# A linear-attention and mixture-of-experts kernel: the mask of the scores ahead of the second operands, another order of loads, and a shorter first layer in two places

## The chip, the cores and the metric

The kernel runs on one core of one Trainium2 chip. The metric is the device time in microseconds (us). Below, PE is the matmul engine, PEld its weight loads, DVE the vector engine, ACT the scalar engine, POOL the GpSimd engine and SP the engine that issues most of the transfers.

## What is computed

A gated recurrence over 4 batches of 768 steps with 8 heads of 48 numbers, then a layer of 8 experts in which each of the 3072 rows goes to the one expert that its gate prefers. Everything is float32.

```python
for t in range(S):                                   # S = 768
    state = alpha[:, :, t, :, None] * state + k[:, :, t] (outer) v[:, :, t]
    y[:, :, t] = q[:, :, t] @ state
x = y as 3072 rows of 384                            # 4 x 768 rows, 8 heads x 48
logits = x @ w_gate                                  # 8 experts
e = argmax(logits); gate = softmax(logits)[e]
out = gate * (relu(x @ w1[e]) @ w2[e])               # w1: 384 x 1024, w2: 1024 x 384
```

## The kernel before, in words

**Attention.** The rows are worked in 24 tiles of 128 steps, six to a batch. For a tile `s` the kernel takes the logarithm of alpha (`logs`, ACT, L326), sums it along the steps with a triangular matmul (`cums`, PE, L337, into one bank named `cum`), and takes two exponentials of the sums on ACT: `icp` (L340) and `cp` (L341, tile `cpb`). `operands` multiplies the keys with `icp` (L360) and the queries with `cp` (L362) into `kqb`, mostly on POOL. `transposes` (PE, L369) turns both, ACT (L374) and DVE (L372) copy them out as `kT` and `qT`. `scores` (PE, L382) makes the 128x128 scores of the even heads in `sA` and of the odd heads in `sB`; DVE masks `sA` into `dA` (L386), ACT copies `sB` into `dB` (L388), and POOL masks `dB` in place (L389). `weighs` (PE, L426) multiplies the scores with the values, `reads` (PE, L414) adds what the state `U` holds, `products` (PE, L448) and `state` (POOL, L463 and L465) carry the state on; no state is carried over the end of a batch, so some passes have half the reads or half the products. `rows` (PE, L474), `keep_rows` (ACT L481, POOL L482) and `store_rows` (SP, L487) turn the result to rows with their gate numbers and write them to DRAM.

The program order is written by hand: each engine runs its instructions in the order in which the code names them. The main loop takes two tiles a pass, `s` = 2, 4, ... 20. A pass takes the results of tiles s and s+1, the logarithms, sums and operands of s+5 and s+6, the transposes of s+3 and s+4, the scores of s+2 and s+3 and the rows of s and s+1. Its second half, in the code's order, ends so:

```python
            more_loads(5)
            do(decay_in, s + 4)
            rows(s + 1)
            keep_rows(s + 1)
            do(operands, s + 6)
            ...
            scores(s + 3)
            store_rows(s)
```

**Loads.** Every load and row store of the loop goes through SP's one queue, in program order. A list `to_load` fixes the order of the loads from tile 7 on; before, it is alpha of tile x+1, keys and queries of tile x, values of tile x-2, over and over. A pass takes 2, 2 and 5 loads from it, with the row stores and small transfers of the decay in between. One load is 192 KB, in pieces of 192 bytes. Keys, queries and alpha have five buffers each, the values six. Below, "k8" is the keys of tile 8, "a10" the alpha of tile 10.

**Routing.** As groups of four tiles are done, `choose` picks each row's expert on DVE, POOL adds up one-hot rows (`ohs`, L500), and two small products on PE (L505 and L506, `rank_products`) give each row its rank within its expert. From these come the lists of rows to gather.

**Experts.** The 8 experts are worked one after the other in 8 places of fixed size, `caps` = 448, 384, 448, 384, 416, 416, 416, 416 rows; expert 0 takes the first place and the others theirs by their counts after 20 tiles (`nth_of`). Rows are gathered in blocks of 128 that may straddle two places (POOL, L269), turned on PE (L960), put through `layer1` (PE, L968: 8 parts of 128 hidden numbers, each over 3 parts of the row, with the place's rows as columns; the relu on DVE and ACT, L973 and L975), and through `layer2` (PE, L984; scaled by the gate on ACT, L989; scattered to the output by POOL, L990). An expert with more rows than its place has all rows past a threshold `XR` done again in extra blocks of 128 rows, in a loop at the end that runs as often as `extra_blocks` counts; `room` holds the places' sizes for that count.

Of the kernel before, what the change touches and what calls it, by code (L numbers as in the profile page):

```python
# [18 lines left out]
def kernel(  # L19
# [29 lines left out]
    nc = tc.nc  # L49
    B, H, S, D = q.shape  # L50
    C = 128
# [21 lines left out]
    nth_of = (5, 0, 6, 1, 2, 3, 4)  # L73
    begins = [sum(caps[:i]) for i in range(E + 1)]
    NBK = begins[-1] // C
    CAP = max(caps)

    XR = min(caps)
    NX = -(-(N - XR) // C)
    assert E == 8 and begins[-1] % C == 0 and NX <= 32 and all(c % UN == 0 and c <= NU * UN for c in caps)  # L80

# [11 lines left out]
    EC = EB * C  # L93
# [82 lines left out]
    def late_consts(i):  # L176
        if i == 0:
            nc.gpsimd.memset(lt_strict[:], 1.0)
            nc.gpsimd.affine_select(
                lt_strict[:], lt_strict[:], compare_op=ALU.is_gt, fill=0.0,  # L180
                base=0, pattern=[[1, C]], channel_multiplier=-1,
            )
            nc.gpsimd.memset(ones_sq[:], 1.0)
        if i == 1:
            nc.gpsimd.memset(zero_e[:], 0.0)
            nc.gpsimd.memset(zero_w[:], 0.0)
        if 2 <= i < 9:
            for ti, tf, pattern, base, mult in list(iotas.values())[2 * (i - 2) : 2 * (i - 1)]:
                n = 1
                for _, m in pattern:  # L190
                    n *= m
                if n < ti.shape[1]:
                    nc.gpsimd.memset(ti[:, n:], -1)
                nc.gpsimd.iota(ti[:, :n], pattern=pattern, base=base, channel_multiplier=mult)
                nc.gpsimd.tensor_copy(tf[:], ti[:])
            if i == 2:
                nc.gpsimd.tensor_copy(ohs[:, 0, :], ohs0[:])
        p = i - 9
        if 0 <= p < E - 1:
            nc.gpsimd.memset(nth[:, p : p + 1], float(nth_of[p]))  # L200
            nc.gpsimd.memset(room[:, p : p + 1], float(caps[p + 1]))

    e_d = nc.dram_tensor("decay_rows", (NT // 2 + 1, 2 * H * DP), F32, kind="Internal").ap()
    x_d = nc.dram_tensor("x_rows", (N + 1, W), F32, kind="Internal").ap()
# [30 lines left out]
    w_t = {}  # L235
# [51 lines left out]
    with tc.tile_pool(name="ld", bufs=6) as ld, \  # L287
# [21 lines left out]
        def some_loads(names):  # L309
# [3 lines left out]

        to_load = [
            (n, x + d) for x in range(7, NT + 2)
            for n, d in ((("a", 1), ("k", 0), ("q", 0), ("v", -2)) * 2)[3 * (x > 7) :][:4]
        ]


# [283 lines left out]
        def do(f, i, *a):  # L603
            if 0 <= i < NT:
                f(i, *a)
# [90 lines left out]
        for s in range(2, NT - 2, 2):  # L696
            more_loads(2)
            if s == 2:
                store_rows(0)
            do(decay_out, s + 4)  # L700
            more_loads(2)

            for _ in range(8 if s > NT - 8 else 0):
                next(parts, None)
            y = results_of(s)
            reads(s)
            reads(s + 1)

            weighs(s, 0)
            weighs(s, 1)  # L710
            products(s + 1)
            products(s + 2)
            weighs(s + 1, 0)
            results_to(s, y, 0)
            weighs(s + 1, 1)
            results_to(s, y, 1)
            state(s + 1)
            do(logs, s + 5)
            if hots:
                one_hots(hots.pop(0))  # L720
            scores(s + 2)
            do(logs, s + 6)
            do(cums, s + 5)
            ranks = y[0][:].rearrange("r i p t -> r (i p t)")
            ranked = [rank_products(g, ranks[:, : len(g) * E]) for g in groups_of if g[-1] == s - 1]
            counts = ranks[:, C : C + E]
            if s in (TE, ORD):

                nc.tensor.matmul(
                    counts, lhsT=ones_sq[:], rhs=ohs[:, s, :], start=True, stop=True, skip_group_check=True,  # L730
                )
            if s == ORD:
                early_slots(ranks[:, 2 * C : 2 * C + EB * NQ])
                fetch_lot(0)
            for r in ranked if s < ORD else ():
                slots_of(*r)
            transposes(s + 3)
            do(operands, s + 5)
            state(s + 2)
            rows(s)  # L740
            keep_rows(s)
            store_rows(s - 1)
            if s == ORD:
                for r in ranked:
                    slots_of(*r)
                key = standing(counts[0:1, :])
                one_hots(hots.pop(0))
                one_hots(hots.pop(0))
                route = rps.tile([C, Dm], F32, name="cum")
                tokens_of_slots(0, TE)  # L750
            do(cums, s + 6)
            do(transposes, s + 4)
            more_loads(5)
            do(decay_in, s + 4)
            rows(s + 1)
            keep_rows(s + 1)
            do(operands, s + 6)
            if s == TE:
                close_early(counts[0:1, 0:1])
            scores(s + 3)  # L760
            store_rows(s)
            if s == 2:

                nc.sync.dma_start(x_d[N // 2 : N // 2 + 1, :], zero_w[:])
            late_consts(s + 2)
            late_consts(s + 3)
            if s == ORD:
                choose(groups_of[-2])
            if hots:
                one_hots(hots.pop(0))  # L770
            for g in groups_of[:-2]:
                if g[-1] == s + 1:
                    choose(g)
            for _ in range(4 if s == NT - 8 else 0):
                next(parts, None)
# [96 lines left out]
    def extra_blocks():  # L872

        cnt = sm.tile([1, E], F32)
        nc.vector.tensor_tensor(cnt[:], tot[:], rank0[:], op=ALU.subtract)
        og = sm.tile([1, E, NX], F32)
        nc.vector.tensor_tensor(
            og[:], cnt[:].unsqueeze(2).to_broadcast([1, E, NX]), thr[:, None, :].to_broadcast([1, E, NX]), op=ALU.is_gt,
        )
        ovt = sm.tile([1, E], F32)  # L880
        nc.vector.reduce_sum(ovt[:], og[:], axis=AX)
        sq = [1, E - 1, E - 1]
        own = sm.tile(sq, F32)
        nc.vector.tensor_tensor(
            own[:], stand[:].unsqueeze(2).to_broadcast(sq), nth[:, None, :].to_broadcast(sq), op=ALU.is_equal,
        )
        nc.vector.tensor_tensor(own[:], own[:], room[:, None, :].to_broadcast(sq), op=ALU.mult)
        cap = sm.tile([1, E], F32)
        nc.vector.memset(cap[:, :1], float(caps[0]))
        nc.vector.reduce_sum(cap[:, 1:], own[:], axis=AX)  # L890
        nc.vector.tensor_tensor(cap[:], cnt[:], cap[:], op=ALU.is_gt)
        nc.vector.tensor_tensor(ovt[:], ovt[:], cap[:], op=ALU.mult)
        ove = sm.tile([1, E], F32)
        nc.vector.tensor_tensor_scan(ove[:], ovt[:], zero_e[0:1, :], 0.0, op0=ALU.add, op1=ALU.add)
        ovs = sm.tile([1, E], F32)
        nc.vector.tensor_sub(ovs[:], ove[:], ovt[:])
        kx_b = kx[0:1, :].unsqueeze(2).to_broadcast([1, NX, E])

        def per(v):
            return v[0:1, None, :].to_broadcast([1, NX, E])  # L900

        ended = sm.tile([1, NX, E], F32)
        nc.vector.tensor_tensor(ended[:], per(ove), kx_b, op=ALU.is_le)
        xf = sm.tile([1, 2 * NX + 1], F32)
        nc.vector.reduce_sum(xf[:, :NX], ended[:], axis=AX)
        nc.vector.tensor_scalar_min(xf[:, :NX], xf[:, :NX], float(E - 1))

        at_x = sm.tile([1, NX, E], F32)
        nc.vector.tensor_tensor(at_x[:], kx_b, per(ovs), op=ALU.subtract)
        live = sm.tile([1, NX, E], F32)  # L910
        nc.vector.tensor_scalar(live[:], at_x[:], scalar1=0.0, scalar2=None, op0=ALU.is_ge)
        nc.vector.tensor_tensor(live[:], live[:], ended[:], op=ALU.subtract)
        nc.vector.tensor_tensor(at_x[:], at_x[:], per(xcol), op=ALU.add)
        nc.vector.tensor_tensor(at_x[:], at_x[:], live[:], op=ALU.mult)
        nc.vector.reduce_sum(xf[:, NX : 2 * NX], at_x[:], axis=AX)
        nc.vector.tensor_copy(xf[:, 2 * NX :], ove[0:1, E - 1 :])
        nc.vector.tensor_copy(xe[:], xf[:])
# [121 lines left out]
    for i in range(E):  # L1039
        if i == 0:  # L1040
            go_ahead(9)
            for k in range(EB, needed[0][-1] + 1):
                turn_block(k)
                go_ahead(3)
            go_ahead(99)
            layer1(w_t[0][0], xT[0], h_t[0], EC, caps[0])
        else:
            if i == E - 1:

                nc.gpsimd.drain()  # L1050
            h_t[i] = (wk if i % 2 else early).tile([C, FB, CAP], F32, name="h_sb", bufs=1)
            layer1(w_t[i][0], xT[i], h_t[i], 0, caps[i])

        coming = list(needed[i + 1]) if i + 1 < E else []
        for k in coming[:2]:
# [75 lines left out]
```

## Time and profile before

| | us |
|---|---|
| time, median of 4 runs (lowest, highest) | 431.84 (431.72, 432.11) |
| the profiled execution: its time | 433.72 |
| the profiled execution: its span in the trace | 431.8 |
| PE busy | 422.4 |
| DVE, ACT, POOL busy | 140.8, 108.4, 140.4 |
| second layer, matmuls (L984) | 137.1 |
| first layer, matmuls (L968) | 125.1 |

A profile is one execution. The busy time of an engine says how full it is, not whether it sets the end: for that one looks at what PE, the fullest one here, waited for. The row of the granted clock (PEclk) tells in tenths at what share of its full speed PE was allowed to run in each fortieth of the span. The attention takes about the first 141 us, the routing and the gathers up to about 160 us, the experts the rest.

### The profile page before, as it was taken

The page shows a single profiled execution, that of the slowest core. Times are in us where ns is not written, and L with a number is a line of the kernel's source. Part 1 is how long each engine was busy: PE and PEld are TensorE (multiplying, and loading weights), DVE is VectorE, ACT ScalarE, POOL GpSimd, SP SyncE. Part 2 cuts the span into 40 slices and gives each one's busy share as a digit, 9 for nine tenths or more (in the row PEclk, how much of TensorE's full clock was granted, in tenths as well). Part 3 has the DMA queues.
Part 4 walks back from the last instruction along what each step waited for, and adds up shares of the span by engine and source line. Part 5 has one row for each costly group of instructions (what it writes and reads, how often), then busy time and mean ns, then how long its engine had stood idle before and what let it go on. Part 6 is the DMA issues. An engine that isn't in the chain of part 4 may idle for free.

```text
span 431.8 us, 7708 instructions
## 1 busy us (share of the span) xinstructions
PE 422.4 (98%) x2990; PEld 286.6 (66%) x2990; DVE 140.8 (33%) x414; ACT 108.4 (25%) x230; POOL 140.4 (33%) x254
## 2 busy tenths in 40 slices
PE   8999899999999999999999999999999999999995
PEld 6887788888889888555555555655655455555452
DVE  6434457575767843721012101201201101111100
ACT  4565354555552321110111111011110110011011
POOL 5395577666655250160160110024010010010011
PEclk9999699999999999999999999999999999999999
DMA  9999999899986232995542710624530050000000
GB/s 158 185 166 199 199 197 187 177 191 194 189 220 204 99 99 80 395 397 170 193 113 58 266 40 10 250 86 120 212 116 18 2 182 20 0 32 20 1 33 29
DMA packets 132576, 59.43 MB, mean 138 GB/s; under 512 B 114614, under 2 KB 127452, under 8 KB 132538
## 3 DMA queue, kind: packets, MB, share of 16 engines
q1 hardware_dynamic: 127720, 48.96, 44.8%
q0 software_dynamic: 3328, 9.94, 7.1%
q8 instruction: 24, 0.39, 0.4%
q10 hardware_dynamic: 1490, 0.02, 0.2%
q14 instruction: 14, 0.11, 0.1%
HBM read 49.32 MB, written 9.98 MB: 137 GB/s over the span
## 4 chain that ended last, share of the span: by engine, by line
PE 63%; issue 28%; POOL 5%; DMA 2%; POOLq 0%; ACT 0%; DVE 0%; SPq 0%; DVEq 0%
PE zp L984 16%; PE hp L968 14%; PE sA L382 6%; PE y L426 5%; PE tp L369 5%; PE xr L474 5%; PE cum L337 4%; POOL out_dram L990 3%; PE y L414 2%; PE xr L612 2%; PE xtp L960 1%; PE sB L448 1%; POOL xg L269 1%; PE hp L785 1%; DMA k_sb<-in_k_dram 1%
## 5 line engine op out<-in xcount | busy, mean ns | idle before, releaser
L984 PE MATMUL zp<-w,h_sb 128*128 128x384 f32 (+2 forms) x560 | 137.1, 487 | 0.0
L968 PE MATMUL hp<-xT,w 128*128 128x416 f32 (+3 forms) x384 | 125.1, 486 | 0.0
L984 PEld LDWEIGHTS zp<-w,h_sb 128*128 128x128 f32 (+2 forms) x560 | 73.6, 163 | 56.3 <-issue 14.8
L968 PEld LDWEIGHTS hp<-xT,w 128*128 128x128 f32 x384 | 71.8, 190 | 51.8 <-issue 37.8
L990 POOL DMA_INDIRECT out_dram<-zo,o_idx x26 | 25.8, 992 | 219.2 <-ACT zo L989 214.2
L973 DVE TENSOR_SCALAR h_sb<-hp 128x416 f32<-128x416 f32 (+3 forms) x32 | 17.9, 558 | 149.2 <-PE hp L968 149.2
L989 ACT ACTIVATE zo<-zp,gw 128x384 f32<-128x384 f32 x26 | 15.1, 580 | 123.7 <-PE zp L984 119.1
L975 ACT ACTIVATE h_sb<-hp 128x416 f32<-128x416 f32 (+3 forms) x32 | 15.7, 490 | 107.3 <-PE hp L968 107.3
L382 PE MATMUL sA<-qT,kT 48*128 48x128 f32 x192 | 28.6, 291 | 0.2 <-DVE qT L372 0.2
L269 POOL DMA_INDIRECT xg<-x_rows,g_idx x26 | 25.1, 965 | 11.1 <-issue 6.4
L382 PE MATMUL sB<-qT,kT 48*128 48x128 f32 x192 | 28.6, 291 | 0.0
L962 DVE COPY xT<-xtp 128x384 f32<-128x384 f32 (+3 forms) x29 | 13.1, 485 | 44.3 <-PE xtp L960 44.2
L426 PE MATMUL y<-dB,vb 128*64 128x128 f32 x192 | 25.5, 279 | 2.1 <-POOL dB L389 2.1
L382 PEld LDWEIGHTS sA<-qT,kT 48*128 48x128 f32 x192 | 24.0, 193 | 4.9 <-issue 2.2
L360 POOL TENSOR_TENSOR kqb<-k_sb,icp 128x384 f32<-128x384 f32 x23 | 23.0, 1000 | 12.0 <-ACT icp L340 8.2
L426 PE MATMUL y<-dA,vb 128*64 128x128 f32 x192 | 26.6, 279 | 0.0
L369 PE MATMUL tp<-ident,kqb 128*128 128x128 f32 x192 | 26.2, 280 | 0.2 <-POOL kqb L362 0.2
L369 PEld LDWEIGHTS tp<-ident,kqb 128*128 128x128 f32 x192 | 22.6, 144 | 5.3 <-issue 2.7
L474 PE MATMUL xr<-back,yT 128*128 128x104 f32 x192 | 25.5, 277 | 0.0
L474 PEld LDWEIGHTS xr<-back,yT 128*128 128x128 f32 x192 | 24.1, 195 | 0.8 <-ACT xs L481 0.2
L382 PEld LDWEIGHTS sB<-qT,kT 48*128 48x128 f32 x192 | 24.0, 193 | 0.0
L372 DVE COPY qT<-tp 128x512 f32<-128x512 f32 x24 | 16.6, 690 | 20.4 <-PE tp L369 20.3
(178 smaller groups left out, 436.6 us busy)
## 6 DMA issues: line engine op xcount, KB each, us to landing
w<-in_moe_w_dram SPq DMA_DIRECT2D x14, 1536.0 KB, 6.7
x_rows<-xs SPq DMA_DIRECT2D x24, 196.0 KB, 3.4
a_sb<-in_alpha_dram SPq DMA_DIRECT2D x24, 192.0 KB, 4.1
k_sb<-in_k_dram SPq DMA_DIRECT2D x24, 192.0 KB, 3.8
q_sb<-in_q_dram SPq DMA_DIRECT2D x24, 192.0 KB, 4.5
vb<-in_v_dram SPq DMA_DIRECT2D x24, 192.0 KB, 3.8
w<-in_moe_w_dram SPq DMA_DIRECT2D x12, 128.0 KB, 4.1
w<-in_moe_w_dram SPq DMA_DIRECT2D x8, 192.0 KB, 3.9
```

The costliest lines, as they stand in the source:

```text
L269: nc.gpsimd.indirect_dma_start(out=xg[:, j, :], out_offset=None, in_=x_d[: N + 1 if n else TE * C + 1, :], in_offset=bass.IndirectOffsetOn ...
L337: nc.tensor.matmul(cum[:], lhsT=cmask[:], rhs=d["ln"][:], start=True, stop=True)
L360: k.tensor_tensor(kq[:, 0, :, :D], d["k"][:], heads(d["icp"]), op=ALU.mult)
L369: nc.tensor.transpose(tp[:, p, :], pair(kqb[s % 4][:, i], p), ident[:])
L372: nc.vector.tensor_copy(d[n][:], tp[:])
L382: nc.tensor.matmul(t[:, p, :], lhsT=d["kT"][r : r + D, p, :], rhs=d["qT"][r : r + D, p, :], start=True, stop=True,)
L426: nc.tensor.matmul(d["y"][h][at(p, a) : at(p, a) + DP, n, :], lhsT=d["v"][:, 2 * p + a, :], rhs=d["d" + "AB"[a]][:, p, :], start=(first an ...
L474: nc.tensor.matmul(xr[:, p, :], lhsT=d["yT"][:, p // (NP // 2), p % (NP // 2), :], rhs=back[:, p, :], start=True, stop=True)
L968: nc.tensor.matmul(hp[:, c0:c1], lhsT=w1[:, a, f * C : (f + 1) * C], rhs=xT[:, a, c0:c1], start=(a == 0), stop=(a == DB - 1),)
L973: nc.vector.tensor_relu(h[:, f, c0:c1], hp[:, c0:c1])
L984: nc.tensor.matmul(zp[i * wd : (i + 1) * wd, :], lhsT=h[:, f, c : c + wd], rhs=w2[:, f, :], start=(f == 0), stop=(f == FB - 1), skip_group ...
L990: ins = nc.gpsimd.indirect_dma_start(out=out[:, :], out_offset=bass.IndirectOffsetOnAxis(ap=idx, axis=0), in_=zo[:], in_offset=None, bound ...
```

## The change

Four things change.

1. In each pass of the loop `operands(s + 6)` stands after `scores(s + 3)`. On POOL the mask of `dB` (L389) of tile s+3 thereby stands ahead of the two products (L360, L362) of tile s+6. It changes the order in the passes s = 2 to 16, in which tiles s+6 are left; no other engine's order changes by it.
2. From tile 8 on the list of loads is keys of x, values of x-2, alpha of x+1, queries of x. From the second row store of the first pass on, SP's loads are then k8, v6, a9, q8, k9, v7, a10, q9, k10, v8, a11, q10, k11, v9, a12, q11, ... in place of v6, a9, k8, q8, v7, a10, k9, q9, v8, a11, k10, q10, v9, a12, k11, q11, ...; how many loads stand between the stores stays the same.
3. A list `cols` holds the columns of the first layer: 368 in the fourth place (of 384) and 400 in the eighth (of 416). The place keeps its gather, its turns and its second layer. POOL sets the hidden rows past the columns to zero ahead of the two first layers.
4. What counts as too many rows for a place is taken from `cols`; the threshold `XR` of the extra blocks goes from 384 to 256, and their greatest number from 21 to 22, so that some constants and the small operations that count the extra blocks get 22 columns in place of 21.

```diff
+    cols = (448, 384, 448, 368, 416, 416, 416, 400)
     CAP = max(caps)
-    XR = min(caps)
+    XR = min(cols) // C * C
     NX = -(-(N - XR) // C)
...
-            nc.gpsimd.memset(room[:, p : p + 1], float(caps[p + 1]))
+            nc.gpsimd.memset(room[:, p : p + 1], float(cols[p + 1]))
...
         to_load = [
             (n, x + d) for x in range(7, NT + 2)
-            for n, d in ((("a", 1), ("k", 0), ("q", 0), ("v", -2)) * 2)[3 * (x > 7) :][:4]
+            for n, d in (
+                (("a", 1), ("k", 0), ("q", 0), ("v", -2)) if x == 7 else (("k", 0), ("v", -2), ("a", 1), ("q", 0))
+            )
         ]
...
             keep_rows(s + 1)
-            do(operands, s + 6)
             if s == TE:
                 close_early(counts[0:1, 0:1])
             scores(s + 3)
+            do(operands, s + 6)
             store_rows(s)
...
-        nc.vector.memset(cap[:, :1], float(caps[0]))
+        nc.vector.memset(cap[:, :1], float(cols[0]))
...
-            layer1(w_t[0][0], xT[0], h_t[0], EC, caps[0])
+            layer1(w_t[0][0], xT[0], h_t[0], EC, cols[0])
...
-            layer1(w_t[i][0], xT[i], h_t[i], 0, caps[i])
+            if cols[i] < caps[i]:
+                nc.gpsimd.memset(h_t[i][:, :, cols[i] : caps[i]], 0.0)
+            layer1(w_t[i][0], xT[i], h_t[i], 0, cols[i])
```

## The prediction, made before the change was run

> **What bounds the kernel now.** I read the page first: the busy row, then the clock row.
>
> ```profile
> PE 422.4 (98%) x2990; PEld 286.6 (66%) x2990; DVE 140.8 (33%) x414; ACT 108.4 (25%) x230; POOL 140.4 (33%) x254
> PEclk9999699999999999999999999999999999999999
> ```
>
> PE is the bound from end to end, so an edit counts only if it removes a hole in PE, a stretch of slow clock, or PE work. One slice, the fifth (43.2 to 54.0 us), has a clock of 0.6. So next PE's own order of time, then the windows around that place (columns: stretch; its length, then busy us of PE, PEld, DVE, ACT, POOL; granted clock; DMA share; GB/s).
>
> ```profile
> 44.57 0.32 PE L426 MATMUL y<-dB,vb 128*64 128x128 f32 x1 [2.06 <-POOL dB L389]
> ```
>
> ```profile
> 43.00:44.00 1.00, 0.00 (x0) 0.00 (x0) 0.00 (x0) 0.13 (x1) 1.00 (x2) 1.00 0.76 183
> 45.00:46.00 1.00, 1.00 (x14) 0.67 (x9) 0.69 (x1) 0.00 (x0) 0.85 (x6) 0.60 0.87 167
> 51.00:52.00 1.00, 1.00 (x6) 1.00 (x6) 0.79 (x2) 0.23 (x1) 1.00 (x2) 0.50 1.01 183
> 52.00:53.00 1.00, 1.00 (x8) 0.82 (x7) 0.33 (x2) 0.11 (x1) 0.71 (x3) 0.99 1.10 208
> ```
>
> PE idles once for 2.06 us (the other holes of the loop are 0.2 us), and after it the clock is 0.5 from 45.2 (0.60 over the slice from 45 means 0.2 us at full) to 52.0: 6.8 us at half speed, 3.4 us lost. Check: from the first weighing matmul of pass s=4 (40.74) to that of s=6 (56.66) are 15.92 us; the same pass shape at s=10 (78.86 to 89.00) takes 10.14, and s=4 has 0.2 us of rank products more. **The prize is 5.6 us**, of which 2.06 + 3.4 are these two. Now POOL's order shows why (start, us, idle before):
>
> ```profile
> 39.52 0.32 POOL L482 COPY xs<-lgn 128x8 f32<-128x8 f32 x2
> 41.98 0.99 POOL L360 TENSOR_TENSOR kqb<-k_sb,icp 128x384 f32<-128x384 f32 x1 [2.14 <-DMA k_sb<-in_k_dram]
> 42.93 0.99 POOL L362 TENSOR_TENSOR kqb<-q_sb,cpb 128x384 f32<-128x384 f32 x1
> 43.88 0.64 POOL L389 TENSOR_SCALAR_AFFINE_SELECT dB<-dB 128x512 f32<-128x512 f32 x1
> ```
>
> The mask of tile 5 stands behind the operands of tile 8, whose keys land at 41.85; ACT had finished copying that dB at 40.44.
>
> **The change, part by part.** *Mask first.* The mask starts at 40.5 and ends at 41.1; PE asks for it at about 42.2 (second weighing at 42.12). The hole of 2.06 goes, with 1 us to spare.
>
> *What is late next: the load order.* SP's rows, the queue as it is (start, issue us):
>
> ```profile
> 36.57 0.39 SPq L304 DMA_DIRECT2D vb<-in_v_dram  x1
> 37.01 0.69 SPq L307 DMA_DIRECT2D a_sb<-in_alpha_dram  x1
> 37.76 0.76 SPq L307 DMA_DIRECT2D k_sb<-in_k_dram  x1
> 38.55 0.88 SPq L307 DMA_DIRECT2D q_sb<-in_q_dram  x1
> 39.54 1.08 SPq L304 DMA_DIRECT2D vb<-in_v_dram  x1
> 40.66 0.95 SPq L351 DMA_DIRECT2D Eb<-decay_rows  x1
> 41.72 0.77 SPq L487 DMA_DIRECT2D x_rows<-xs  x1
> 42.54 0.29 SPq L764 DMA_DIRECT2D x_rows<-zero_w  x1
> 42.87 0.38 SPq L307 DMA_DIRECT2D a_sb<-in_alpha_dram  x1
> 43.29 1.08 SPq L307 DMA_DIRECT2D k_sb<-in_k_dram  x1
> ```
>
> The DMA share is about 1.0 here, so landings follow the places in this queue; by the trace's landing events the load places land at 39.5, 40.9, 41.9, 42.7, 43.4, 46.2 and 47.4. Before they hold v6, a9, k8, q8, v7, a10, k9; after: k8, v6, a9, q8, k9, v7, a10. No issue is added and none changes its buffers' owners, so I let the places keep their times. Then, with PE undelayed: k8 (39.5) is there before the mask ends; v6 at 40.9 serves the products of tile 6 at 41.67; a9 at 41.9 serves its logarithm at 42.60. **But a10 moves from 46.2 to 47.4, and nobody stalls ahead of it now.** Its logarithm stands on ACT ahead of icp and cp of tile 9 (pass s=10: ln at 82.94, cp done at 84.22, 1.28 later). So cp of tile 9 is done at 47.45 + 1.28 = 48.7, and the next cumulative matmul needs both that ln and the bank that cp frees: 48.8. Undelayed, PE reaches it at 40.74 + (84.81 - 78.86) + 0.2 = 46.9. **PE waits 1.9 us.** Inside the same 1.9 lies another wait: the rank product (at 4.7 us after the weighing in s=12, 0.45 less here for one products group: 44.95) needs POOL's sums L500. They stand behind q8 (lands 42.7, done 43.75) and the iotas (44.47 to 45.84 before, 1.37 us), so three of the four sums end at 45.9: 1.0 us. So about 1.0 us idle before the transposes and 0.9 after, 2 us of matmuls between.
>
> *Does the clock drop for that?* The trace has 2.06 us (dropped) and 0.41 us (150.16, not dropped). Each piece, 0.9 to 1.0, is nearer to 0.41; I take no drop, and keep 3.4 us as the other end. The Trainium skill, "TensorE: Matmul & The Clock Gate", section "Why this matters for your kernels", asks only that no idle gap exceed about 3 us. By it neither the old hole nor the new ones would cost clock; the trace's 2.06 us hole did, so that rule is not leaned on; taken alone it gives the sum that I forecast.
>
> So the attention phase gives 5.6 - 1.9 = **3.7 us**. Its bounds: if a10 comes early the sums still hold PE 1.0 (4.6), without both 5.6; with a clock drop 0.3.
>
> *Other loads, with PE 3.7 earlier.* a12 was used at 61.21, now 57.5, and moves from the end of the second group to the first place after the row store of tile 4: about 56.6 (the old landing of k11, 57.4, less the 0.8 that SP waited for that store). Spare 0.9. k and q of 11 and 12, a11, v8 have 1 us and more (a11: 52.0 against 55.3). From s=8 on passes of 10.1 to 11.1 us need some 10 us of DMA, and SP already waits for row stores (1.6 us at 63.8, 2.3 at 91.8), so no load binds. Cost 0; if a12's cover goes, its lateness is paid on PE.
>
> *Mask first in the other seven passes.* POOL now waits for ACT's dB (s=10: 89.19) before the operands of s+6, so its last operand ends at 91.8 where the old mask ended at 90.42. The transposes of that tile come 4 us or more later. Tightest are the rank sums ahead of s=8: done 70.82 for a product at 72.39; 0.95 later leaves 0.6. Cost 0, covered by PE's products and scores; without the cover, up to 1.4 us in a pass.
>
> *First layer, 368 and 400 columns.* From the chain of waits, 384 against 448 columns:
>
> ```profile
> 184.29 15.48 PE hp L968 x48
> 216.54 18.04 PE hp L968 x48
> ```
>
> 2.56 us for 64 columns, 0.04 a column and layer: 2 x 16 x 0.04 = **1.28 us**, all on PE, which has no hole in this phase. The evictions shrink too, off the path. Two memsets of 128x128 elements are added on POOL (the nearest row, the 128x128 f32 memset of a constant, took 0.20 us). The first stands behind the scatter that ends at 258.43, and DVE's first eviction of that place starts at 258.48: it may slip 0.2, while three hp banks give PE 3.6 us. The second follows the drain ending at 390.98, likewise. Behind them are only scatters that wait for zo anyway. Cost 0.
>
> *Extra blocks.* Counting the reference's choices, the two places take experts 3 (354 rows, 368 columns) and 2 (356 rows, 400), and the others fit too: no extra block runs. The rest of the threshold change is 22 columns for 21 on one partition of DVE (some 10 instructions of 0.32 us, 5% longer, off the path) and 0.03 us in POOL's iotas.
>
> **Sum.** 3.7 + 1.28 = 4.95 us. Against the profiled execution, 433.7 (span 431.8 and 1.9 around it that nothing here touches): 428.8. The runs' median, 431.84, is 1.9 below that execution; the same difference gives **426.9**.
>
> **Rivals.** (1) *The clock drops again* after the two waits: 6.8 us at half speed, 3.4 lost: 430.3. For it: 1.9 us of idling within 3.9 us, close to 2.06. Against: in any 3.4 us stretch at most 1.5 of it. (2) *No wait is left*: alpha early and the sums hidden: 5.6 + 1.28 = 6.9: 425.0; for the sums alone 425.9. Against it: the full DMA queue. (3) *Slower: alpha decides.* With a drop, the place is still the ln of tile 10: each us that a10 lands after 47.4 is a us of PE. The gain of 6.9 is used up at 1.9 + 3.4 + 1.6, so from a landing at 49.0 on the kernel is slower; if a10 slips two places of about 1.1 us, 49.6, it is 432.4, and with a12 late behind it up to 433. For it: the same queue drives every load of these passes. Against: loads land within 0.4 us of their places' rhythm. (4) *The change does not act*: the stall returns whole at another load and only the columns remain: 430.6; it lies with (1).
>
> **How the numbers follow.** Forecast (with a margin of 0.8) 0.52; clock drop or returned stall, (1) and (4), 0.20; no wait, (2), 0.12; slower by more than 0.2%, (3), 0.11; cancelling to within 0.2% 0.05. A measurement of this kernel can tell some 0.2%, 0.9 us. Faster: 0.52 + 0.20 + 0.12 = 0.84. The range takes in the forecast, (2) and (1) with (4): 424.8 to 430.8.
>
> **What would show it.** Right: no PE wait for dB L389; PE waits near 45 and 48 us, for ohs L500 and for ACT's ln or cp; the ln of tile 10 waiting for in_alpha at 47.4; a clock row without a 6; the layers at the two places 0.64 us shorter. Wrong: a 6 or 7 in the clock row at the fifth or sixth slice (rival 1), PE waits for alpha or operands after 56 us (rival 3), a second stretch of PE work after the last scatter (extra blocks).

## The result, and the profile after

The changed kernel takes **430.51 us** (median of 52 runs) against 431.59 for the kernel before beside it (median of 78 runs). The ratio is 0.9971 with a 95% interval of 0.9963 to 0.9979: by it the change is 1.25 us faster (the medians differ by 1.08) where 4.9 was forecast. The profiled execution took 432.01 us, near the slow end of its kernel's runs (429.70 to 432.49); its span is 430.2.

The page of the changed kernel, its busy row and its clock row:

```profile
PE 418.7 (97%) x2990; PEld 284.0 (66%) x2990; DVE 142.0 (33%) x414; ACT 108.1 (25%) x230; POOL 141.5 (33%) x256
PEclk9999999999999999999999999999999999999998
```

PE is busy 3.7 us less, and the 6 of the fifth slice is gone. The shorter columns account for 1.26 us of the 3.7 (below); most of the rest goes with the clock, since in three other profiles of the kernel before, all at full clock, PE is busy 419.8 to 420.5 us in place of 422.4. The windows of the changed kernel (columns as in the prediction) show the full clock, and in the first of them a DMA share of 0.23:

```profile
45.00:46.00 1.00, 1.00 (x10) 0.55 (x7) 1.00 (x3) 0.58 (x1) 0.79 (x7) 1.00 0.23 39
51.00:52.00 1.00, 1.00 (x11) 1.00 (x10) 0.21 (x1) 1.00 (x3) 1.00 (x3) 1.00 1.04 210
```

POOL's order in the changed kernel shows the mask of tile 5 (L393) ahead of the operands of tile 8, at 41.59 in place of 43.88:

```profile
41.59 0.63 POOL L393 TENSOR_SCALAR_AFFINE_SELECT dB<-dB 128x512 f32<-128x512 f32 x1 [1.10 <-ACT dB L392]
42.20 1.01 POOL L364 TENSOR_TENSOR kqb<-k_sb,icp 128x384 f32<-128x384 f32 x1
43.36 1.01 POOL L366 TENSOR_TENSOR kqb<-q_sb,cpb 128x384 f32<-128x384 f32 x1 [0.16 <-DMA q_sb<-in_q_dram]
```

PE's waits in the changed kernel (who waited for whom: us in total, times, longest):

```profile
PE cum L341 <- ACT cpb L345: 2.3, 2, 1.5
...
PE sA L386 <- DVE accA L458: 1.1, 2, 0.7
...
PE tp L373 <- DVE qT L376: 0.4, 1, 0.4
PE y L509 <- POOL ohs L504: 0.3, 1, 0.3
```

The wait for the mask is gone. The first and last rows are waits that the prediction named; the second and third, PE's scores behind DVE's `accA` and its transposes behind DVE's `qT`, are not in it. PE's own order puts a time to those that were named (the row `cum` also holds a wait of 0.83 us in pass s=2):

```profile
46.49 0.18 PE L509 MATMUL y<-ohs,ones_sq 128*128 128x32 f16 x1 [0.29 <-POOL ohs L504]
...
49.97 0.59 PE L341 MATMUL cum<-ln,cmask 128*128 128x384 f32 x1 [1.49 <-ACT cpb L345]
```

and ACT's shows that the second of them is alpha of tile 10, which lands at 48.55:

```profile
48.64 0.52 ACT L330 ACTIVATE ln<-a_sb 128x384 f32<-128x384 f32 x1 [2.63 <-DMA a_sb<-in_alpha_dram]
49.07 0.47 ACT L344 ACTIVATE icp<-cum 128x384 f32<-128x384 f32 x1
49.44 0.48 ACT L345 ACTIVATE cpb<-cum 128x384 f32<-128x384 f32 x1
```

So the wait for alpha came as forecast and the time did not. A table of the passes says where it went: the us from the first weighing matmul of a pass to that of the next, from PE's own order of time, and in the column "rest" the us from the weighing of s=22 to the end of PE's last matmul. The passes not shown agree to 0.02 us in these six. The name "again" is a second profile of the same kernel.

| profile | s=2 | s=4 | s=8 | s=12 | s=16 | rest | PE idle in s=4 |
|---|---|---|---|---|---|---|---|
| before | 11.05 | 15.92 | 11.14 | 11.14 | 10.26 | 284.41 | 2.06, then the clock |
| before again (e1) | 11.05 | 11.99 | 11.14 | 11.14 | 10.26 | 284.40 | 1.33 |
| before again (e13) | 11.05 | 11.69 | 11.14 | 11.14 | 10.26 | 284.48 | 1.03 |
| before again (e14) | 11.05 | 11.89 | 11.14 | 11.14 | 10.26 | 284.42 | 1.23 |
| after | 12.12 | 12.43 | 11.61 | 11.96 | 11.06 | 283.15 | 0.29 and 1.49 |
| after again (e5) | 11.05 | 10.63 | 11.61 | 11.95 | 11.07 | 283.06 | 0.09 |

Two things stand out. The profiled execution of before was not like the others: without the clock's drop pass s=4 takes 11.7 to 12.0, not 15.92. And the changed kernel pays in three passes that were forecast at no cost, the same in both of its profiles: 0.47 + 0.81 + 0.80 = **2.08 us**. The 12.12 of s=2 (a wait of 0.83 for alpha of tile 8, whose place the change does not move) is in one profile of the two and is left out of what follows.

### The profile page after: what moved, and what is told of

The parts are those of the page before. It is cut to its first block, busy times and chain, and to the rows that moved or that the text cites. A ratio compares the mean times of both kernels' runs of the same rounds, so it can differ in the third digit from the quotient of the medians.

```text
span 430.2 us, 7702 instructions
## 1 busy us (share of the span) xinstructions
PE 418.7 (97%) x2990; PEld 284.0 (66%) x2990; DVE 142.0 (33%) x414; ACT 108.1 (25%) x230; POOL 141.5 (33%) x256
## 4 chain that ended last, share of the span: by engine, by line
PE 55%; issue 28%; POOL 4%; DVE 4%; DMA 4%; SPq 2%; ACT 1%; POOLq 0%; DVEq 0%; ACTq 0%
PE zp L988 16%; PE hp L972 14%; PE sA L386 5%; PE xr L478 4%; PE tp L373 4%; PE y L430 3%; POOL out_dram L994 3%; PE cum L341 3%; DMA a_sb<-in_alpha_dram 2%; PE xr L616 2%; SPq L309 2%; PE y L418 1%; PE xtp L964 1%; POOL xg L271 1%; DMA Eb<-decay_rows 1%
## 5 line engine op out<-in xcount | busy, mean ns | idle before, releaser
L972 PE MATMUL hp<-xT,w 128*128 128x416 f32 (+5 forms) x384 | 123.9, 483 | 0.0
L977 DVE TENSOR_SCALAR h_sb<-hp 128x416 f32<-128x416 f32 (+5 forms) x32 | 17.7, 554 | 148.1 <-PE hp L972 148.1
L979 ACT ACTIVATE h_sb<-hp 128x416 f32<-128x416 f32 (+5 forms) x32 | 15.6, 487 | 106.1 <-PE hp L972 106.1
L386 PE MATMUL sA<-qT,kT 48*128 48x128 f32 x192 | 27.7, 285 | 1.4 <-DVE accA L458 1.1
L386 PE MATMUL sB<-qT,kT 48*128 48x128 f32 x192 | 27.7, 285 | 0.0
L386 PEld LDWEIGHTS sA<-qT,kT 48*128 48x128 f32 x192 | 23.1, 187 | 6.0 <-issue 1.9
L341 PE MATMUL cum<-ln,cmask 128*128 128x384 f32 x48 | 20.9, 517 | 2.3 <-ACT cpb L345 2.3
```

What stands on the lines that cost most here:

```text
L341: nc.tensor.matmul(cum[:], lhsT=cmask[:], rhs=d["ln"][:], start=True, stop=True)
L386: nc.tensor.matmul(t[:, p, :], lhsT=d["kT"][r : r + D, p, :], rhs=d["qT"][r : r + D, p, :], start=True, stop=True,)
L972: nc.tensor.matmul(hp[:, c0:c1], lhsT=w1[:, a, f * C : (f + 1) * C], rhs=xT[:, a, c0:c1], start=(a == 0), stop=(a == DB - 1),)
L977: nc.vector.tensor_relu(h[:, f, c0:c1], hp[:, c0:c1])
```

## The experiments

The expectations name their theories by letters. **A:** the profiled execution of before was typical. **B:** it was worse than the usual one, so that the prize of 5.6 us was too large. **C:** in the three long passes POOL's products, now beside the choice of experts on DVE, slow it; the rival of C is that the new order of loads makes these passes long. **D:** B and C together. The expectations of e3 and e4 call the three passes 6, 10 and 14, after the pass at whose end the experts are chosen; here they are s=8, 12 and 16, as they are timed.

### Before again (e1, and later e13 and e14)

No edit.

> The kernel before, unchanged, to see how much one execution differs from the next. Theory A (the profiled execution of before was typical): again one hole of about 2 us in PE at the mask of tile 5, the clock at half for about 6.8 us after it, a pass s=4 of about 15.9 us, and alpha of tile 8 in time for pass s=2 (11.05 us). Theory B (that execution was worse than the typical one, so that the prize of 5.6 us was too large): the hole is smaller or the clock does not drop, pass s=4 is 12 to 14 us, and the mean clock of most executions is above 0.995. Time: no difference, 0.

Measured: 430.5 us, ratio to before 0.9999 [0.998, 1.0018]. PE's order and the clock row of this profile:

```profile
45.12 0.32 PE L426 MATMUL y<-dB,vb 128*64 128x128 f32 x1 [1.33 <-POOL dB L389]
```

```profile
PEclk9999999999999999999999999999999999999999
```

The hole is there, 1.33 us, and no slice of the clock drops, as B has it. e13 (430.85 us) and e14 (430.26, one run each beside 430.26 of before) have holes of 1.03 and 1.23, without a drop. The hole follows the keys and queries of tile 8, as e14 expected: in before, e1, e14 and e13 the product of the queries starts 2.19, 1.46, 1.36 and 1.16 us after the weighing of s=4, and the holes are 2.06, 1.33, 1.23 and 1.03.

> The kernel before once more, for its hole alone. By theory B (the profiled execution was worse than the typical one) pass s=4 takes 10.5 to 12.5 us with a hole of 0 to 2 us at the mask and no drop of the clock; by theory A 15.9 us.

> As the one before it: a third look at the hole. The hole should follow the landing of the keys and queries of tile 8 against the time at which PE reaches the weighing of tile 5: the later they land, the longer.

In the 87 runs of before that stood beside the experiments the mean granted clock was 0.991, as in the profile of before (433.72 us), in 3 (433.9, 433.9, 434.2 us), 0.994 in 6, and above 0.995 in 78 (median 430.36 us, highest 432.23). So the usual prize in pass s=4 is 11.7 to 12.0 less the 10.34 of an undisturbed pass, **1.4 to 1.7 us**, not 5.6. In the 78 runs beside the result the clock is not on record; 18 of them took over 432.5 us, against 6 of these 87, so the drop may have been more frequent there.

### One part at a time (e2, e3, e4)

e2: the columns alone (`cols`, `XR`, `room`, `cap`, the fills). e3: the mask alone. e4: the load list alone.

```diff
 # e3
             keep_rows(s + 1)
-            do(operands, s + 6)
...
             scores(s + 3)
+            do(operands, s + 6)
 # e4
-            for n, d in ((("a", 1), ("k", 0), ("q", 0), ("v", -2)) * 2)[3 * (x > 7) :][:4]
+            for n, d in (
+                (("a", 1), ("k", 0), ("q", 0), ("v", -2)) if x == 7 else (("k", 0), ("v", -2), ("a", 1), ("q", 0))
+            )
```

> Only the columns of the first layer (368 and 400), with the zeroed rest and the threshold of the extra blocks. Both theories: 1.28 us faster than before (two layers of 0.64 us less on PE), the attention phase as before. A rival, that the two memsets on POOL hold the relus up, gives less than 0.7.

> Only the mask ahead of the second operands, in all passes, with the old order of loads. Alpha of tile 10 keeps its place (46.2), so PE waits about 1 us in pass s=4 and the pass takes 11 to 11.6 us. Theory C (POOL's products, now beside the choice of experts on DVE, slow it): passes s=6, 10 and 14 are 0.4 to 0.8 us longer, 2.1 in all, as in the changed kernel. Its rival (the longer passes come from the order of loads): these passes as before. Against before: with A and C 2.5 us faster; with B and C 0 to 1 us faster; with B alone 2 to 3 us faster.

> Only the new order of loads, the mask still behind the second operands. The mask of tile 5 then waits for the queries of tile 8, which keep their place (42.7), so the hole in PE stays at 1.9 to 2.0 us and the time within 0.5 us of before. If the keys alone were what held the mask, the hole would shrink to 1 us or less and the kernel would gain 1 to 4 us. Under C passes s=6, 10 and 14 are as before.

| | us (before 430.36) | ratio to before | s=4 | s=8, 12, 16 | rest |
|---|---|---|---|---|---|
| e2 columns | 428.23 | 0.9949 [0.9931, 0.9967] | 10.48 | 11.14, 11.14, 10.26 | 283.20 |
| e3 mask | 431.36 | 1.0018 [1.0005, 1.0030] | 10.49 | 11.60, 12.05, 11.08 | 284.61 |
| e4 loads | 430.41 | 0.9997 [0.9984, 1.0011] | 11.36 | 11.14, 11.14, 10.26 | 284.49 |

The rival of C falls: the loads alone leave the three passes as they were (and keep a hole of 0.60 us at the mask, where 1.9 to 2.0 was expected). The mask alone removes the hole (10.49) and has the three long passes; it was expected 0 to 1 us faster under B and C and is 0.8 us *slower*. Its waits of PE:

```profile
PE sA L382 <- DVE accA L454: 1.1, 2, 0.7
```

And the columns alone gain 2.1 us, more than the whole change and more than their matmuls (284.41 - 283.20 = 1.21); they also have no hole in s=4, which none of these theories explains. That is taken up below.

### What happens in the three passes

After scores(s+3) DVE runs `choose` in the passes that end a group of four tiles, and `accA` stands behind it. DVE's order in the changed kernel, pass s=8 (start, us):

```profile
65.75 0.17 DVE L496 TENSOR_REDUCE lmin<-lgn 128x4 f32<-128x32 f32 x1
65.95 0.81 DVE L498 TENSOR_TENSOR sc<-lgn,lmin 128x32 f32<-128x32 f32 x1
66.80 0.93 DVE L499 TENSOR_TENSOR sc<-sc,first_w 128x32 f32<-128x32 f32 x1
...
68.20 0.35 DVE L458 TENSOR_TENSOR accA<-sA,Ub 128x192 f32<-128x192 f32 x1
```

POOL's order in the same stretch, and PE's:

```profile
65.72 1.00 POOL L364 TENSOR_TENSOR kqb<-k_sb,icp 128x384 f32<-128x384 f32 x1
66.68 1.01 POOL L366 TENSOR_TENSOR kqb<-q_sb,cpb 128x384 f32<-128x384 f32 x1
```

```profile
68.60 0.37 PE L386 MATMUL sA<-qT,kT 48*128 48x128 f32 x1 [0.40 <-DVE accA L458]
```

The two comparisons, 32 numbers wide, end at 66.76 and 67.73; POOL's two products end at 66.72 and 67.69. Each comparison lasts until the product beside it is done. In the kernel before the products stood ahead of the mask and had ended at 68.05, and there the same two comparisons are short (POOL, then DVE):

```profile
67.05 1.00 POOL L362 TENSOR_TENSOR kqb<-q_sb,cpb 128x384 f32<-128x384 f32 x1
```

```profile
67.39 0.75 DVE L575 TENSOR_SCALAR oh_r<-iota_r,rc 128x129 f16<-128x129 f32 x1
...
68.85 0.19 DVE L494 TENSOR_TENSOR sc<-lgn,lmin 128x32 f32<-128x32 f32 x1
69.07 0.19 DVE L495 TENSOR_TENSOR sc<-sc,first_w 128x32 f32<-128x32 f32 x1
...
69.63 0.35 DVE L454 TENSOR_TENSOR accA<-sA,Ub 128x192 f32<-128x192 f32 x1
```

So the new place of the products puts them beside `choose`: 0.62 + 0.74 us more there. Before, the last product lengthens `oh_r` ahead of `choose` instead (0.75 us, in the changed kernel 0.28), so `accA` is not 1.36 but 0.99 us later: it starts 2.90 us after the first weighing of the pass, before 1.91. PE, which needs `accA` out of the bank of `sA` for its next scores, stands 0.40 us in s=8 and 0.75 us in s=12. In s=16 no `accA` is due; there the choice is late by 0.88 us, the ranks follow it, and PE's transposes wait 0.37 us for DVE's `qT` behind them. The Trainium skill, "SBUF — State Buffer", section "SBUF: two separate sides", says it as a rule: DVE and GpSimd share one pair of ports under an exclusive lock, and of a DVE operation with two operands in SBUF and a GpSimd operation that reads SBUF, the one that starts first holds the pair for its whole length. The rows of the two comparisons agree with it; the prediction had looked for what waits for POOL's results and not for what waits for its port.

### The same place, with other work of POOL (e9, e10)

If POOL's reading products hold `choose`, they must do so from any source. The kernel before got useless work of POOL in the passes before a `choose`, at the place where the changed kernel has the operands.

```diff
             scores(s + 3)
+            if s in (6, 10, 14):
+                for _ in range(3):                                   # e9
+                    nc.gpsimd.tensor_tensor(scr[:, : 2 * C], still[:], still[:], op=ALU.mult)
+            if s in (6, 10, 14):
+                for _ in range(4):                                   # e10, alone
+                    nc.gpsimd.memset(scr[:], 0.0)
```

> The kernel before, with three useless POOL products of 128x256 (into a scratch tile nobody reads) after the mask at the end of passes s=6, 10 and 14; nothing else moves. Theory D (a POOL product holds a DVE operation on two SBUF inputs until it ends): DVE's two comparisons of the choice (L494 and L495 of before, 0.19 us each) take 0.5 to 0.9 us, each ending with a POOL product, and passes s=8, 12 and 16 grow by 0.2 to 0.8 us each. Rival (the passes grew because POOL's later work was late): the comparisons stay at 0.19 us.

> As the one with extra products, but four POOL memsets of 128x512 f32 in their place, some 0.54 us each, about the same POOL time. If only POOL operations that read SBUF hold DVE, the comparisons stay at 0.19 us and the passes as before; if every POOL operation holds it, they take 0.4 to 0.6 us each as beside the products. If POOL's lateness were the cause, the passes would grow as much as with the products whatever the comparisons take.

Measured, one run each beside 430.73 of before: e9 431.1 us, e10 432.99. In e9 the passes s=8, 12, 16 take 11.14, 12.06 and 10.26. DVE's order in e9, `choose` of the first two groups, and POOL's products there (0.66 us each):

```profile
65.32 0.42 DVE L495 TENSOR_TENSOR sc<-lgn,lmin 128x32 f32<-128x32 f32 x1
65.78 0.19 DVE L496 TENSOR_TENSOR sc<-sc,first_w 128x32 f32<-128x32 f32 x1
...
87.10 0.42 DVE L495 TENSOR_TENSOR sc<-lgn,lmin 128x32 f32<-128x32 f32 x1
87.56 0.66 DVE L496 TENSOR_TENSOR sc<-sc,first_w 128x32 f32<-128x32 f32 x1
```

```profile
65.09 2.05 POOL L764 TENSOR_TENSOR scr<-still 128x256 f32<-128x256 f32 x3
...
86.87 1.99 POOL L764 TENSOR_TENSOR scr<-still 128x256 f32<-128x256 f32 x3
```

Every lengthened comparison ends with one of them: 65.74 with the first (65.09 + 0.68), 87.52 and 88.22 with the first and second (87.53, 88.20). Where the delay was 0.23 (s=8) PE lost nothing, where it was larger (s=12) PE waited:

```profile
PE sA L383 <- DVE accA L455: 0.9, 1, 0.9
```

So the mechanism is shown: the comparisons grow in all three passes (in s=16 by 0.23 again), where the rival named in the expectation leaves them at 0.19. It costs PE time only in s=12. In e10, whose fills read nothing, the comparisons keep their 0.19 us (DVE, then POOL):

```profile
65.83 1.14 DVE L577 TENSOR_SCALAR oh_c<-iota_h,rc,tokv 128x129 f16<-128x129 f32 x1
66.42 0.55 DVE L493 TENSOR_REDUCE lmin<-lgn 128x4 f32<-128x32 f32 x1
67.03 0.19 DVE L495 TENSOR_TENSOR sc<-lgn,lmin 128x32 f32<-128x32 f32 x1
67.25 0.19 DVE L496 TENSOR_TENSOR sc<-sc,first_w 128x32 f32<-128x32 f32 x1
```

```profile
66.36 2.28 POOL L764 MEMSET scr<- 128x512 f32 x4
```

But a fill is not free either: `oh_c`, 0.66 us in before, took 1.14, and it and the reduction queued behind it end at 66.97, with the first fill (four in 2.28 us from 66.36 on: 66.93). So half of the expectation missed: the passes s=8, 12, 16 are not as before but take 11.27, 11.53 and 11.06. In s=16 the late choice brings `rc_i` and `rc` (1.00 and 0.92 us) beside the regular products. The 1.76 us hole of its s=4 is before's own, and here too the clock stays.

### Undo the cost: mask first in some passes only (e5 to e8, e11, e12)

e5 is the changed kernel once more. e6 is the changed kernel with the old order of mask and operands in the passes s=6, 10 and 14; s=2 keeps the mask first, although a group is chosen at its end too. e7 and, again, e11 are the kernel before with the columns and the mask first in pass s=2 alone (old loads); e8 and e12 are e7 with the loads from tile 8 on in the order alpha, values, keys, queries.

```diff
-            do(operands, s + 6)
+            if not (s == 2 or s % 4 == 0):      # e7, e8: if not (s == 2)
+                do(operands, s + 6)
...
             scores(s + 3)
+            if s == 2 or s % 4 == 0:            # e7, e8: if s == 2
+                do(operands, s + 6)
```

> The changed kernel, unchanged, beside the others of this group. Theory D: against the typical execution of before (a hole of 0 to 2 us without a drop of the clock) it loses 2.0 us to the choice of experts being held on DVE (passes s=8, 12 and 16, timed from weighing to weighing, 0.4 to 0.8 us longer each), gains the hole and 1.28 us of columns: 0.5 to 1.5 us faster than before. Alpha of tile 10 costs 0 to 1.8 us in pass s=4, by how late the loads run in that execution.

> The changed kernel, but in the three passes at whose end experts are chosen and operands of a later tile are left (s=6, 10, 14) the operands of s+6 stay ahead of the scores; mask first in s=2, 4, 8, 12, 16. Theory D (POOL's products hold DVE's choice): passes s=8, 12 and 16 are back at 11.14, 11.14 and 10.26 and the kernel is 2.0 us faster than the changed one. Rival: the longer passes come from mask first as such (late operands, state or sums on POOL), then at least half of the 2.0 stays, since five of the eight passes still have it.

> Mask first in pass s=2 alone, the old order of loads, the shorter columns. Theory D: no hole at the mask, no longer pass: 1.28 us and the hole of before (0 to 2 us, mean about 1) faster than before: 1.8 to 2.8 us, the best so far. If the new order of loads is worth something of its own, the kernel with the split masks is faster than this one; I expect it 0 to 1 us slower, by the wait for alpha of tile 10.

> As the one with mask first in pass s=2 alone, but loads in the order alpha, values, keys, queries from tile 8 on, so that a10 lands two places earlier than in the changed kernel. Under theory D nothing waits in pass s=4 but perhaps the rank sums (0.3 us): the same as with the old order within 0.3 us, or faster by up to 0.5 where loads run late.

> Mask first in pass s=2 alone, old loads, shorter columns, once more beside the next one: 2.5 to 3.3 us faster than before. In its first trace pass s=12 took 11.98 us against 11.14 in before, with DVE's rc_i and rc (0.94 and 0.85 us) held by POOL's products of that pass: by theory D this depends on how the two fall together and may be gone in another execution.

> As the one beside it, with loads in the order alpha, values, keys, queries. If the order of loads matters little, within 0.5 us of it; if it was truly slower by 0.9 us as in the first pair of medians, again 0.6 us or more slower.

| | us | before beside it | ratio to before | s=4 | s=8, 12, 16 |
|---|---|---|---|---|---|
| e5 after again | 429.86 | 430.49 | 0.9976 [0.9955, 0.9997] | 10.63 | 11.61, 11.95, 11.07 |
| e6 split | 427.78 | 430.49 | 0.9925 [0.9897, 0.9952] | 10.64 | 11.14, 11.98, 10.26 |
| e7 mask in s=2 | 427.45 | 430.49 | 0.9921 [0.9890, 0.9951] | 10.50 | 11.14, 11.98, 10.26 |
| e11 the same | 427.70 | 430.73 | 0.9920 [0.9896, 0.9945] | 10.59 | 11.14, 11.14, 10.26 |
| e8 alpha first | 428.34 | 430.49 | 0.9940 [0.9920, 0.9960] | 10.49 | 11.14, 11.14, 10.26 |
| e12 the same | 428.25 | 430.73 | 0.9934 [0.9908, 0.9959] | 10.49 | 11.14, 11.14, 10.26 |

e6 against e5 is the one edit that matters, and it is worth 2.1 us; the intervals do not overlap. In its profile s=8 and s=16 are back as expected, s=12 is not (below). DVE's comparisons in e6, pass s=8, with POOL's products over at 62.98:

```profile
61.97 1.01 POOL L365 TENSOR_TENSOR kqb<-q_sb,cpb 128x384 f32<-128x384 f32 x1
```

```profile
63.77 0.19 DVE L497 TENSOR_TENSOR sc<-lgn,lmin 128x32 f32<-128x32 f32 x1
64.00 0.20 DVE L498 TENSOR_TENSOR sc<-sc,first_w 128x32 f32<-128x32 f32 x1
```

In s=2 the collision is there and costs little: in e7 the comparisons take 0.56 and 0.93 us, and pass s=4 takes 10.50. In s=12, e6 and e7 still had the long pass in their profiles, where `rc_i` (0.94 us in e7) and `rc` (0.85), two later operations of `choose`'s chain, met products that stand where they always stood. In e11, the same kernel as e7, only `rc` did (0.93, `rc_i` 0.17), and the pass is as before. So the kernel before is itself near this collision. e6, e7 and e11 beat both kernels; among these and e8, e12 the intervals overlap. No load order gained anything: alpha first was 0.9 and 0.55 us slower by the medians.

### Why the columns gain 2.1 us (e2, e15, e16, then e17 and e18)

e15 and e16 repeat e2 (one run each beside 430.26 of before).

> The shorter columns alone, once more. Their first run was 2.1 us faster than before where PE's work is 1.25 us shorter; its trace had no hole at the mask. If the rest of 0.8 us is a hole that happened to be small, holes of 0.5 to 2 us show up here as in the kernel before; if the columns' kernel for some reason loads earlier, the hole is again 0 and its loads are a microsecond ahead.

> As the one before it: a third look at the columns' kernel, with the same two readings.

428.15 and 427.55 us, s=4 at 10.24 and 10.33, no hole: it was no accident. The DMA view of the first 12 us (queue, packets, MB, their time as a share of 16 engines) shows the difference before any row is worked, first before, then e2:

```profile
q1 hardware_dynamic: 9658, 1.83, 96.0%
```

```profile
q1 hardware_dynamic: 10851, 2.05, 87.9%
```

Share x 16 x 12 us / packets is the mean time of one packet: 19.1 ns before, 15.6 with the columns. All profiles divide so: 15.3 to 15.8 in the kernels that have the columns, 19 to 19.4 in those that have not. Nothing in the columns' part touches these loads but the layout: 22 columns for 21 make some constants longer, and by the programs' addresses the buffers of alpha, keys and queries (and the first weights and the working tiles) stand 32 bytes further, on a multiple of 64 (154240 for 154208 for the first alpha buffer). So the last two runs move them by a constant of 32 bytes: e17 in the kernel before, onto the multiple of 64; e18 in the columns' kernel, off it.

```diff
+    pad = consts.tile([C, 8], F32)
...
             nc.gpsimd.memset(zero_w[:], 0.0)
+            nc.gpsimd.memset(pad[:], 0.0)
```

> The kernel before with one more constant of 128x8 numbers (32 bytes a partition, filled once during the start), which moves the buffers of the alpha, key and query loads and of the first weights by 32 bytes, on a multiple of 64. Nothing is left out. If the place of the buffers sets the duration of a packet: packets of the first 12 us take some 15.5 ns in place of 19 to 20, the hole of pass s=4 falls from 1.0 to 1.8 us to under 0.4, the stretch from the weighing of s=22 stays at 284.4, and the time is 0.8 to 1.5 us below the kernel before. If not: packets of 19 to 20 ns, a hole of 1.0 to 1.8 us, and no difference (within 0.3 us).

> The kernel before with the columns of the first layer alone and one more constant of 128x8 numbers, which moves the buffers of the alpha, key and query loads and of the first weights back to 32 bytes past a multiple of 64. Nothing is left out. If the place sets it: packets of 19 to 20 ns, the hole of pass s=4 is back with 1.0 to 1.8 us, the stretch from the weighing of s=22 stays at 283.2, and the gain over the kernel before is only the matmuls' 1.25 us. If something else in the columns' part sets it: packets of 15.5 ns, no hole, and a gain of 2.1 us as with the columns alone.

| | buffers past a multiple of 64 | us (before 430.31) | ratio to before | ns a packet | s=4 | rest |
|---|---|---|---|---|---|---|
| e17 before, moved | 0 | 429.45 | 0.9972 [0.9957, 0.9987] | 15.3 | 10.24 | 284.47 |
| e18 columns, moved | 32 | 429.35 | 0.9971 [0.9957, 0.9986] | 19.2 | 10.75 | 283.29 |

The DMA view of e17, then of e18:

```profile
q1 hardware_dynamic: 11106, 2.10, 88.5%
```

```profile
q1 hardware_dynamic: 10341, 1.96, 103.5%
```

Thirty-two bytes turn the mean packet of the first 12 us from 19.1 to 15.3 ns and back, and with it 0.9 us of the kernel before (forecast 0.8 to 1.5) and about 1.1 of the columns' gain, which falls from 2.1 to 1.0 (the matmuls' 1.25 by forecast; the intervals of e2 and e18 still overlap a little). The way to the hole shows beside e1 and e13, whose first weighing starts when that of e17 does (16.36 to 16.38): the keys of tile 8 land at 40.54 in e17, at 42.39 and 42.08 in those. One item of e18 missed: its profiled execution, the fastest of its twelve runs, has a hole of only 0.09 us where 1.0 to 1.8 was expected, though the time says that its runs lose on average as the others do. The slow packets are those of one stretch: in all the kernels with buffers off the multiple of 64 the 192-byte packets take 21.4 to 22.6 ns between 4 and 10 us (15.3 to 16.2 in the others), but up to 4 us there is no difference, and from 28 to 60 us they take 16.0 to 16.5 against 15.4 to 15.8. Why 32 bytes matter to a packet of 192, and why most in that stretch, is not shown.

## Why the prediction was wrong, point by point

- **"The prize is 5.6 us": wrong, the largest miss.** It is right for the profiled execution and not for the kernel. In three other profiles the prize is 1.4 to 1.7: the hole is 1.0 to 1.3 and the 3.4 us of half clock do not follow. The page had given a sign: this execution took 433.72 us where the four runs lay between 431.72 and 432.11. The sum carried that excess of 1.9 us over unchanged (428.8 to 426.9), as if it had nothing to do with the prize. It goes with the drop: in the experiments' runs of before the three at a mean clock of 0.991 took 433.9 to 434.2 us, the 78 at full clock 430.36 in the median.
- **"Mask first in the other seven passes: cost 0": wrong.** 2.08 us in passes s=8, 12 and 16, by e3 (which has them from the mask alone), e6 and e9. The step followed POOL's results to their users, and priced the missing cover at 1.4 us a pass; the cost came over DVE, whose two comparisons (0.19 us each) last until the POOL product beside them is done (0.81 and 0.93).
- **Mask first in s=2: right.** The hole goes (e3: 10.49).
- **"a10 moves to 47.4, PE waits 1.9": right in the profile after, not in general.** By the weighing of s=4, at 41.82 there and 40.74 before, a10 landed 6.73 us behind it (forecast 6.66), PE waited 0.29 + 1.49 = 1.78 us, and the pass was 3.49 us shorter than the profiled one of before (forecast 3.7). The parts were not the forecast ones: 0.29 for the sums, not 1.0, and 1.49 for alpha, not 0.9. In e5 it landed 4.3 behind the weighing and cost nothing. So the match is luck in part: the loads of the profiled execution after ran late (alpha of tile 8 landed at 35.69 us, in e5 at 31.99), and the DMA share fell to 0.23 from 45 to 46 us where the step took about 1.0.
- **No clock drop: right.** Idle times of 1.78 us in two pieces (after) and of 1.76 (e10), 1.33 and 1.23 in one left the clock at full; one of 2.06 did not. The rule of the Trainium skill, "TensorE: Matmul & The Clock Gate", section "Why this matters for your kernels", no idle gap over about 3 us, would have allowed that one too.
- **Other loads, cost 0: right** in the kernels with the new order (after, e4, e5, e6): PE has no wait after 56 us that a load of these explains.
- **Columns, 1.28 us: right.** The rest of the span shrank by 1.26 (284.41 to 283.15), the layer by 0.64:

```profile
256.20 14.84 PE hp L972 x48
```

- **Memsets 0, no extra blocks: right.** "22 columns for 21 ... off the path" was wrong in a way that no instruction shows: those bytes move the load buffers, for 0.9 us (e17).

What makes the sum: -1.25 for the columns' matmuls, some -1.3 for the hole (the packets alone remove it, and so does the mask alone, and it can go only once; e3's time has +2.08 less 1.3 = 0.8), +2.08 in the three passes: -0.5. Measured were -1.25 [-1.6, -0.9] and, in e5's group, -1.0 [-1.9, -0.1]. The remaining 0.5 to 0.8 us is not assigned; PE's first weighing alone starts up to 1.3 us apart in executions of one kernel. The rivals named a clock drop, early alpha, late alpha and a returned stall; the new wait was none of them. That the time lies beside those of rivals (1) and (4), 430.3 and 430.6, is chance: no clock dropped and no stall returned.

## What to carry to other kernels

Before costing a hole and what follows it, see whether the profiled execution's own time lies among the unprofiled runs; if it is above them by about what the hole costs, price the change by a usual execution. When a POOL instruction that reads two tiles is moved, look at DVE's instructions in its new stretch, not only at its users: there a comparison of 0.19 us took up to 0.93, and keeping the old order in the three passes where that cost PE time was worth 2.1 us. And a change that alters the size of any constant may move every buffer behind it: compare packet times before crediting the edit.

## What the runs showed of the hardware that was not expected

- Packets of 192 bytes took 21.4 to 22.6 ns on average between 4 and 10 us into buffers that start 32 bytes past a multiple of 64, and 15.3 to 16.2 ns in the same stretch into buffers on a multiple of 64 (e17, e18 and all others). From 28 to 60 us they took 16.0 to 16.5 against 15.4 to 15.8.
- PE's first weighing starts between 15.09 and 16.38 us in four executions of the kernel before. It goes with the moment at which the granted clock first reaches full: 4.23, 5.56, 7.30 and 7.35 us stand beside 15.09, 15.64, 16.38 and 16.38.
- A hole of 2.06 us was followed by 6.8 us of half clock, holes of 1.76 us and less in other executions by none. In every trace the clock changes at moments that lie whole multiples of 3.41 us apart (before: 4.23, 45.19 and 52.02). Counted from the first change, the 2.06 us lie within one such stretch (41.78 to 45.19), while the 1.76 us of e10 are split by a boundary at 44.44 into 0.73 and 1.03. So the same hole may drop the clock in one execution and not in the next; with one drop among the traces this is not shown.
